# One routed-attention and SoLU kernel, its hand-written order rewritten from the first scores on

## The chip, the cores and the metric

The kernel runs on one core of one Trainium2 chip. The metric is device time in microseconds (us) of one execution; the runs of the kernel before gave 222.96, 223.10 and 223.19, median 223.1. A profiled execution gives the instruction times that are used below.

## What is computed

```python
q_n, k_n, c_n = (each row divided by its norm)             # q, k, v: 4 x 8 x 768 x 64, centroids: 8 x 16 x 64
q_assign = argmax(q_n . c_n);  k_assign = argmax(k_n . c_n)   # 16 clusters a head
scores = (q @ k^T) / 8, and -1e9 where q_assign != k_assign
attn = softmax(scores) @ v                                  # -> x: 3072 tokens x 512
h = x @ w_in                                                # 512 -> 1024
solu = h * softmax(h)
ln = (solu - mean) / sqrt(var + 1e-6) * g_ln
out = ln @ w_out                                            # 1024 -> 512, float32
```

## The kernel before

There are 16 pairs of heads, written b.p (batch 0 to 3, pair 0 to 3). The mask is put into the score matmul: the 64 rows of q and k of a head get 16 more rows, the one-hot cluster of each token, so that a score in the right cluster is raised by a constant and the others vanish in the exponential. The rows of q and k with their one-hot rows stand in the tiles qk0 to qk5.

The kernel is a list of small steps with names. Those that matter here:

- ld, lv: loads of q or k, and of v (DMA, issued from SyncE's queue). ld2.1.1 is k of pair 2.1.
- tp and xa (pairs of batch 0 only): TensorE turns a tile of q or k, and VectorE or ScalarE copies it out of PSUM (L409). xt (the other batches): VectorE turns it (L427).
- ca b.p.i.hh: cast of q (i = 0) or k (i = 1) of one head of the pair to bf16 into qk; L453 or L455 on GpSimd and VectorE, L451 on ScalarE.
- cl, tb, mx, oh, ot: the clusters of a pair. A matmul gives the 16 products of each token (cl, L465 or L470), VectorE turns them back (tb, L479), takes the maximum (mx, L492), compares (oh, L504, for pairs 0.1 to 0.3 L498) and turns the result (ot, L514 or L511). For a pair of batch 0 these four follow each other on VectorE and each takes the result of the one before.
- pl b.p.i.part: four copies of that result into the one-hot rows of qk (L534, for pairs 0.1 to 0.3 L526). bl: a memset beside it (L543). cv: a cast of v (L552).
- S, E, V, N: scores of a bank of up to 512 columns (TensorE, L621), their exponential (ScalarE, L627), the product with v (TensorE, L644), the division by the sum (VectorE, L656 and L669). A unit of three banks is named by one number: S8.0, S8.1 and S8.2 are unit 8, the first of pair 0.3; unit 4 is the first of pair 0.1, unit 6 of pair 0.2. Three PSUM banks hold scores, so each S waits for the E three banks before; the first S of a pair also waits for its ca and pl.
- h, hm, ex, u, tu, y, bn, ag, at, al, sc, ou: the second half of the network for a tile of 128 tokens: x @ w_in (L730), maximum, exponential, product, turn by DMA, product with w_out (L794), variance, the scale on GpSimd (at, al), scaling of the result (sc, on ScalarE L809 or VectorE L811), store.
- su, sk, me, ce: w_out is centred once, early; su is one us of matmuls (L593).

The order on each engine is a table of words: a word is a kind of step and how many of that kind come next, and a word with = names one step out of its turn. AWAY names the steps that go to another engine than their kind's default. Each engine works through its list strictly in order, so that a step that waits holds everything behind it on its engine. `run` walks the five lists, and every step issues its instructions when its turn comes; semaphores between engines follow from the tiles.

```python
ORDER["SP"], ORDER["POOL"], ORDER["PE"], ORDER["DVE"], ORDER["ACT"]   # the five lists
first, eng = eng, self.AWAY.get(name, eng)                             # the engine of a step
```

Of the kernel before, what the change touches and what calls it, by code (L numbers as in the profile page):

```python
# [22 lines left out]
class Weave:  # L23
# [11 lines left out]
    ORDER["POOL"] = """
        po z ca2 pl2 cv bl zo =pl0.0.1.0.0 pl bl ca2 cv z ca2 cv =pl0.1.1.1 z pl ca =pl0.1.0.1 pl ca
        gs =ca0.3.0.1 =pl0.2.0.0 pl =ca0.3.1.0 pl ca pl cv pl z cv wi sg =wi2 wi2 =pl1.0.0.0
        =pl1.0.1.1 =ca1.0.0.1 ca2 =pl1.0.0.1 pl =ca1.1.1.1 bl =ca1.1.0.1 cv =ca1.1.1.0 pl2 at z cv
        al =cv1.1.1 =pl1.1.0.1 ca cv pl ca at al at =ca1.2.1.0 =pl1.2.1.1 =cv1.3.0 =pl1.2.0.0
        =ca1.2.1.1 pl2 al cv bl ca2 cv =ca1.3.1.0 at =ca2.0.0.0 =ca1.3.1.1 al ca =pl1.3.0.0  # L40
        =pl1.3.1.1 pl at pl ca2 pl =pl2.0.0.0 =pl2.0.0.1 pl al cv at ca cv =pl2.1.0.0 =ca2.2.0.0 al
        =ca2.1.1.1 =pl2.1.1.1 =ca2.2.1.1 =ca2.1.1.0 ca =ca2.3.1.1 at pl2 at al bl cv ca at
        =ca2.2.1.0 =pl2.2.1.1 pl =pl2.2.0.1 =cv2.2.0 cv pl bl ca =ca3.0.0.1 al2 at =pl2.3.1.1
        =ca3.0.1.1 ca =ca2.3.1.0 =pl2.3.0.0 =ca3.0.1.0 pl bl at ca =pl3.0.0.1 al cv =pl3.0.1.1 ca
        pl2 bl =ca3.1.1.0 cv ca cv =pl3.1.1.1 =ca3.2.0.1 al at al =ca3.3.0.0 =pl3.1.0.1 cv pl bl pl
        ca2 =pl3.2.0.1 ca =ca3.3.1.1 at al ca =cv3.3.0 =cv3.2.1 =cv3.3.1 at pl cv pl bl =pl3.3.0.1
        pl ca bl at al at al at3 al4 at3 al at al2 at al2
    """
    ORDER["PE"] = """
        wm tp fl3 cp fl2 tp2 cl tp fl10 cl fl8 S2 tp S cq tp S tp S tp S tp S2 tp S cl V S V2 S2 tp2  # L50
        S2 V3 tp S tp S tp S2 cl S2 V S V2 S gt S tp S3 V S V2 S cl S3 su S V S V2 S2 V S3 V2 S V2
        S3 V2 S2 V S V S cl S3 su S3 V3 S V S me S V S V S V2 S3 V2 S2 V2 S2 h S h S2 V S V h S V S
        V S h S2 h S V2 S V S V h S cl S V2 S h S V S2 V h S2 h S h S2 V3 S2 V3 S2 y3 S y S h S h S
        V3 S cl V S2 h2 S V2 S2 h S h S2 V2 S V S V S y V2 y S y2 h S h S2 V2 y S3 y2 S V S2 V3 S y
        S2 h S h cl S3 V4 S V y V S2 y h S y V S y h S3 V cl S V S V2 S2 V S h S h V S V3 S3 cl S2
        V2 y2 S y S V2 S2 y S V S h2 S h S V S h S V S V h y2 S3 V y V S h S h S y V h S3 V2 cl S h
        V h S cl S h S V2 S V2 S V S h S2 h V S h S y2 S2 V3 S y V S2 V S y h V S2 h S y S V2 S V S2
        h V y2 S2 V2 h S y S2 h2 V S2 V S cl V S V S V2 S h2 S cl S2 V S y V S V S y V y S2 V h y S
        h S2 cl S V S2 y4 V2 S2 V2 S y S2 V3 S V S y S2 y V S2 V2 S V S h S h S V S2 V h y S h S V S
        V S V S V h2 S y V S y S V S V S h S2 V h S V S V S y2 h S h S V S cl h S h S V2 S2 h S V2 h  # L60
        S y V y S2 h2 S2 V4 S h V h S y S V S y S2 h S h S V3 S h V S h y V S y S V S h S h S2 V S V
        y h S2 V2 y h V2 S3 h2 S2 V S V2 y2 S V S y h y h2 S h S2 V2 h V S V y S y S h y2 h2 S2 V y
        S y3 V h2 y h2 y3 V2 h2 y4 h2 ptx y4 h2 y3 h2 ptu y ptu y6 ptu y ptu y5
    """
    ORDER["DVE"] = """
        cn cb xa ca tb mx oh ot pl2 tb mx oh ot xa pl xa cf xa ca2 tb mx pl oh ot xa N xa cv tb mx
        oh gk ot xa pl N tb mx oh ot pl N cv pl cv N xt2 ca N tb mx oh sk ot N ce2 N ce4 N ce2 xt N
        hm xt N u tb mx oh N ot hm bn2 xt ag bl u N xt hm tb bn u bn N mx ag oh bn hm ot cv N sc u
        bn2 ag xt bn xt ag xt N hm tb mx oh xt N ot xt u bl bn xt tb N bn hm N mx tb oh ag ot u N xt
        mx oh bl ot bn hm N bn ag u xt2 bn hm xt tb u N tb mx cv oh bn ag hm N ot mx bn u oh bn ot N  # L70
        bn hm xt ag bn xt u ag N xt bn hm tb xt N mx tb oh ot u bn xt ag xt hm tb N mx cv mx u N oh
        bn oh N bn ot bn2 ag N ot xt hm ag sc N u bn2 ag xt hm N sc u ca tb bn hm mx oh u ot N hm bn
        ag bn u cv N bn hm N ag u bn hm N bn2 u N ag sc hm bn2 ag u bn N hm ag bn2 u bn ag N hm bn
        ag u bn2 hm sc N u ag bn2 hm tx ag sc u bn2 hm tu sc ag u2 bn2 ag sc2
    """
# [16 lines left out]
    AWAY.update(dict.fromkeys("""  # L92
        pl0.0.0.1.0 pl0.0.1.0.0 pl1.0.0.0 pl1.0.0.1 pl1.0.1.0 pl1.0.1.1 pl1.1.0.0 pl1.1.0.1
        pl1.1.1.0 pl1.1.1.1 pl1.2.0.0 pl1.2.0.1 pl1.2.1.0 pl1.2.1.1 pl1.3.0.0 pl1.3.0.1 pl1.3.1.0
        pl1.3.1.1 pl2.0.0.0 pl2.0.0.1 pl2.0.1.0 pl2.0.1.1 pl2.1.0.0 pl2.1.0.1 pl2.1.1.0 pl2.1.1.1
        pl2.2.0.0 pl2.2.0.1 pl2.2.1.0 pl2.2.1.1 pl2.3.0.0 pl2.3.1.0 pl2.3.1.1 pl3.0.0.0 pl3.0.0.1
        pl3.0.1.0 pl3.0.1.1 pl3.1.0.1 pl3.1.1.0 pl3.1.1.1 pl3.2.0.0 pl3.2.0.1 pl3.2.1.0 pl3.3.0.1
        pl3.3.1.0 pl3.3.1.1
    """.split(), "POOL"))
# [1180 lines left out]
```

## Time and profile before

| | |
|---|---|
| median of three runs | 223.1 us |
| the profiled execution's own time | 223.39 us |
| its span (first to last instruction) | 221.2 us |
| granted TensorE clock over the span | 0.997 |
| TensorE busy | 213.0 us, 96% |
| VectorE busy | 198.8 us, 90% |
| ScalarE busy | 194.0 us, 88% |
| GpSimd busy | 126.7 us, 57% |

In rows of the profile PE is TensorE's matmul, PEld its weight loads, DVE is VectorE, ACT ScalarE, POOL GpSimd, SP SyncE; L621 is line 621 of the kernel before. A row of the timeline has start, duration, engine, line, operation, what is written from what, how often, and in square brackets the idle time before it with what ended it. Three engines are nearly full, so the question in each stretch is which of them the others wait for. A matmul's end is modelled, so that a busy TensorE is not always TensorE at its peak.

### The profile page before, as it was taken

The numbers are of one execution on the slowest core, as the hardware profiler recorded it, in microseconds if no ns is written. First come the engines' busy times: TensorE is split into PE (matmuls) and PEld (weight loads), VectorE is DVE, ScalarE is ACT, GpSimd is POOL, SyncE is SP. The second block draws the span as 40 slices with busy tenths as digits, with TensorE's granted clock in tenths as the row PEclk, the third lists the DMA queues.
The fourth block names the chain that finished last, engine by engine and source line by source line (L and its number), as shares of the span: only waits on it lengthen the run. The fifth ranks groups of instructions, "written<-read, shape, count | busy, mean of one in ns | idle before, by whom it ended". The sixth has DMA issues, their size and how long they took to land.

```text
span 221.2 us, 6638 instructions
## 1 busy us (share of the span) xinstructions
PE 213.0 (96%) x2421; PEld 142.3 (64%) x2454; DVE 198.8 (90%) x354; ACT 194.0 (88%) x379; POOL 126.7 (57%) x245
## 2 busy tenths in 40 slices
...
GB/s 158 327 281 239 208 358 257 149 131 170 140 214 174 193 148 133 193 192 155 209 206 133 177 127 211 220 166 179 269 114 61 48 122 190 117 100 158 176 71 142
DMA packets 125679, 38.80 MB, mean 175 GB/s; under 512 B 115016, under 2 KB 121168, under 8 KB 125648
## 3 DMA queue, kind: packets, MB, share of 16 engines
...
q10 hardware_dynamic: 1744, 0.52, 1.0%
q8 instruction: 19, 0.31, 0.6%
...
## 4 chain that ended last, share of the span: by engine, by line
PE 79%; SPq 4%; DVE 4%; DMA 4%; POOL 2%; ACT 2%; issue 2%; POOLq 0%; DVEq 0%; ACTq 0%
PE sps L621 25%; PE hreg L730 17%; PE yps L794 16%; PE ops L644 14%; PE csc L470 4%; SPq L421 3%; DMA raw<-in_k_dram 2%; ACT e L627 2%; DMA raw<-in_q_dram 2%; PE hreg L402 1%; SPq L418 1%; POOL qk L526 1%; POOL qk L453 1%; PE hreg L794 1%; DVE cst L479 1%
## 5 line engine op out<-in xcount | busy, mean ns | idle before, releaser
L627 ACT ACTIVATE e<-sps 128x512 bf16<-128x512 f32 (+1 forms) x294 | 150.9, 601 | 6.5 <-PE sps L621 4.9
L621 PE MATMUL sps<-qk 80*128 80x256 bf16 (+5 forms) x636 | 99.0, 262 | 1.1 <-POOL qk L526 0.4
L621 PEld LDWEIGHTS <-qk 80*128 80x128 bf16 (+1 forms) x636 | 50.7, 97 | 34.3 <-issue 9.2
L644 PEld LDWEIGHTS <-e 128*128 128x128 bf16 x1152 | 51.6, 97 | 11.7 <-issue 1.9
L644 PE MATMUL ops<-v,e 128*128 128x65 bf16 x1152 | 56.9, 193 | 0.4 <-DVE x L669 0.4
L730 PE MATMUL hreg<-w_in_sb,xT 128*128 128x512 bf16 x176 | 51.2, 378 | 0.9
L794 PE MATMUL yps<-w_out_c,uT 128*128 128x512 bf16 x167 | 46.5, 378 | 0.9
L742 ACT ACTIVATE e_sb<-hreg,nmax 128x1024 bf16<-128x1024 f32 x24 | 26.9, 1122 | 8.0 <-DVE nmax L736 7.9
L736 DVE TENSOR_REDUCE nmax<-hreg 128x1 f32<-128x1024 f32 x24 | 29.1, 1213 | 4.7 <-PE hreg L730 4.6
L760 DVE BATCH_NORM_STATS2 bs<-u 128x6 f32<-128x512 bf16 x48 | 31.5, 676 | 0.2
L534 POOL COPY qk<-oht 32x384 f32<-32x384 f32 (+1 forms) x48 | 23.9, 498 | 12.7 <-DVE oht L514 8.7
L749 DVE TENSOR_TENSOR u<-e_sb,hreg 128x1024 bf16<-128x1024 bf16 (+1 forms) x25 | 29.1, 1167 | 1.2 <-ACT e_sb L742 1.0
L453 POOL CAST qk<-xt 64x768 bf16<-64x768 f32 (+1 forms) x30 | 24.5, 818 | 5.7 <-DVE xt L409 3.4
L455 POOL TENSOR_SCALAR qk<-xt 64x768 bf16<-64x768 f32 x26 | 21.8, 838 | 8.0 <-DVE xt L427 6.3
L794 PEld LDWEIGHTS <-uT 128*128 128x128 bf16 x200 | 18.1, 97 | 11.1 <-issue 0.3
L776 POOL TENSOR_SCALAR esq<-es,mv 128x1 f32<-128x1 f32 x24 | 8.9, 370 | 27.4 <-DVE mv L764 23.8
L427 DVE STREAM_TRANSPOSE xt<-raw 128x768 f32<-128x768 f32 x24 | 22.8, 956 | 0.9 <-DMA raw<-in_k_dram 0.9
L730 PEld LDWEIGHTS <-xT 128*128 128x128 bf16 x192 | 17.0, 97 | 8.7 <-DVE u L749 1.0
L669 DVE TENSOR_TENSOR x<-ops,den 128x256 bf16<-128x256 f32 (+1 forms) x39 | 18.9, 486 | 1.3
L770 POOL TENSOR_SCALAR es<-esum 128x1 f32<-128x1 f32 x24 | 5.9, 247 | 24.0 <-ACT e_sb L742 23.3
L552 POOL CAST v<-vf 128x384 bf16<-128x384 f32 x25 | 12.8, 518 | 3.8 <-DMA vf<-in_v_dram 3.0
L779 POOL TENSOR_TENSOR alpha<-esq,halves 128x1 f32<-128x1 f32 x24 | 13.6, 568 | 2.0
...
## 6 DMA issues: line engine op xcount, KB each, us to landing
...
```

The source lines that it names most:

```text
L427: nc.vector.transpose(xt[:], raws[b, p, i][:].rearrange("p j c -> p (j c)"))
L453: VEC[e].tensor_copy(dst, src)
L534: ins = VEC[e].tensor_copy(dst.bitcast(F32), src.bitcast(F32).unsqueeze(1) .to_broadcast([NB, 2, n // 2]))
L621: nc.tensor.matmul(sps_[n, k][:, c0:c0 + w], side(b, h // 2, 1, h % 2, keys)[r], side(b, h // 2, 0, h % 2, slice(s0 * P, s0 * P + w))[r])
L627: nc.scalar.activation(es[n, k][:, :w], sps_[n, k][:, :w], Act.Exp, scale=exp_scale, bias=-exp_scale)
L644: nc.tensor.matmul(opss[g][:, s, :VW], es[n, k][:, c0:c0 + P], v1[slot(b, h // 2)][:, h % 2, kt, :VW], start=(kt == 0), stop=(kt == n_t - 1))
L730: uses(nc.tensor.matmul(hreg[:, at(f, f2)[1], :], xTs[f][:, dc, :], w_in_sb[:, dc, f2 * FF2:(f2 + 1) * FF2], start=(dc == 0), stop=(dc == ...
L736: uses(nc.vector.tensor_reduce(ff[f, "nmax"][:], pair_of(f), axis=AXY, op=Alu.max, negate=True), *both(f))
L742: uses(nc.scalar.activation(ff[f, "e"][:], pair_of(f), Act.Exp, bias=ff[f, "nmax"][:], accum_out=ff[f, "esum"][:]), *both(f))
L749: uses(nc.vector.tensor_tensor(ff[f, "u"][:, at_], ff[f, "e"][:, at_], pair_of(f)[:, at_], op=Alu.mult), *banks)
L760: nc.vector.bn_stats(ff[f, "bs"][:, f2, :], ff[f, "u"][:, f2, :])
L794: ins = nc.tensor.matmul(dst, ff[f, "uT"][:, at(f, f2)[0] * (n_fc // 2) + c, :], w_out_c[:, fc, cols], start=(fc == chunks[0]), stop=(fc = ...
```

## The change

The five lists and AWAY are new; steps, buffers, tile sizes and the rules of waiting are the same. All five lists begin as before: TensorE's up to S0.1, VectorE's up to tb0.0.1 (at 9.45 us in the profile), ScalarE's up to E0.2, GpSimd's first six steps, SyncE's first 16. They also end as before: TensorE's from S90.0, VectorE's from N32, ScalarE's from E74.0 on. What moves between engines can be read in AWAY, from which the lines that differ are these (a step that is not named has its default engine: GpSimd for ca of whole tiles, cv, bl and the pl of pairs 0.1 to 0.3; VectorE for xa outside pair 0.0; ScalarE for sc).

```diff
     ORDER["POOL"] = """
-        po z ca2 pl2 cv bl zo =pl0.0.1.0.0 pl bl ca2 cv z ca2 cv =pl0.1.1.1 z pl ca =pl0.1.0.1 pl ca
+        po z ca2 pl2 =z4 bl zo sg cv pl bl ca =ca0.1.1.1 ca =z3 ca pl cv ca z pl =ca0.3.0.1 gs cv
...
     AWAY.update(dict.fromkeys("""
-        ca0.0.0.0.0 ca0.0.0.1.1 ca0.3.1.1 ca3.3.1.0 sc23.0 tu22.1 tu23.1 xa0.0.1.0 xa0.1.0.1
-        xa0.2.0.0 xa0.2.0.1 xa0.2.1.0 xa0.2.1.1 xa0.3.1.0
+        ca0.0.0.0.0 ca0.0.0.1.1 ca1.3.0.1 ca2.1.0.1 ca2.2.1.1 ca3.3.1.0 sc23.0 tu22.1 tu23.1
+        xa0.0.1.0 xa0.1.0.1 xa0.2.0.0 xa0.2.0.1 xa0.2.1.0 xa0.2.1.1 xa0.3.0.0
     """.split(), "ACT"))
     AWAY.update(dict.fromkeys("""
-        bl1.1 bl1.3 bl2.0 ca0.0.1.0.0 ca0.1.0.0 ca0.1.1.0 ca1.0.1.0 ca3.1.0.1 cv0.1.1 cv0.2.1
-        cv0.3.0 cv1.2.1 cv2.2.1 cv2.3.0 cv3.2.0 pl0.0.0.0.1 pl0.0.1.0.1 pl0.2.1.0 pl0.3.0.0
-        pl0.3.0.1 sc1 sc10 sc11 sc13 sc17 sc19 sc20 sc22 sc23.1 tu22.0
+        bl1.0 bl3.0 ca0.0.1.0.0 ca0.1.0.0 ca0.2.0.1 ca0.2.1.0 ca1.1.1.1 ca3.1.0.1 cv0.0.0 cv0.2.0
+        cv0.2.1 cv0.3.0 cv1.2.0 cv1.3.1 cv2.3.0 cv3.0.1 pl0.0.0.0.1 pl0.0.1.0.1 pl0.1.0.0 pl0.1.0.1
+        pl0.2.1.0 pl0.3.0.0 sc1 sc10 sc11 sc13 sc17 sc19 sc20 sc22 sc23.1 sc5 tu22.0
     """.split(), "DVE"))
```

Numbers behind a name in the rows below are buffer numbers; a line number of the kernel after is one less than that of the kernel before.

VectorE, pairs 0.1 and 0.2, before: from oh0.1 (the compare) and ot0.1 (the turn) to ot0.2.

```order
L498 TENSOR_TENSOR w_out_c_113<-cst_386,mx_406 128x12x2x16
L511 STREAM_TRANSPOSE w_out_c_113<-w_out_c_113 128x768
L409 COPY xt_469<-hreg_111 128x384
L656 RECIPROCAL den_480<-ops_378 128x6
L669 TENSOR_TENSOR x_479<-ops_378,den_480 128x2x3x64
L409 COPY xt_469<-hreg_111 128x384
L552 CAST v1_1_106<-vf_232 128x6x64
L479 STREAM_TRANSPOSE cst_513<-csc_496 128x384
L492 TENSOR_REDUCE mx_530<-cst_513 128x24
L498 TENSOR_TENSOR w_out_c_113<-cst_513,mx_530 128x12x2x16
L581 COPY g_ln2_115<-gps_549 128x8
L511 STREAM_TRANSPOSE w_out_c_113<-w_out_c_113 128x768
```

VectorE, the same stretch after: oh0.1 is the line behind mx_409, and its oh0.2 follows behind these rows.

```order
L491 TENSOR_REDUCE mx_409<-cst_392 128x24
L497 TENSOR_TENSOR w_out_c_113<-cst_392,mx_409 128x12x2x16
L452 CAST qk2_101<-xt_380 64x6x128
L510 STREAM_TRANSPOSE w_out_c_113<-w_out_c_113 128x768
L655 RECIPROCAL den_473<-ops_385 128x6
L668 TENSOR_TENSOR x_472<-ops_385,den_473 128x2x3x64
L408 COPY xt_485<-hreg_111 128x384
L525 COPY qk1_100<-w_out_c_113 16x2x3x64
L408 COPY xt_504<-hreg_111 128x384
L525 COPY qk1_100<-w_out_c_113 16x2x3x64
L478 STREAM_TRANSPOSE cst_527<-csc_495 128x384
L454 TENSOR_SCALAR qk2_101<-xt_435 64x6x128
```

Between the turn of pair 0.1 and the turn back of pair 0.2 the cast of v is gone, and two pl of pair 0.1 stand there; two casts of pair 0.2 stand inside the chain of four.

GpSimd, the same stretch before: from the first cast of pair 0.2 to the last pl of pair 0.2.

```order
L453 CAST qk2_101<-xt_375 64x6x128 x2
L552 CAST v1_1_106<-vf_232 128x6x64
L526 COPY qk1_100<-w_out_c_113 16x2x3x64
L1245 MEMSET v1_3_108 128x12x2
L526 COPY qk1_100<-w_out_c_113 16x2x3x64
L455 TENSOR_SCALAR qk2_101<-xt_433 64x6x128
L526 COPY qk1_100<-w_out_c_113 16x2x3x64 x2
L455 TENSOR_SCALAR qk2_101<-xt_433 64x6x128
L587 COPY w_out_c_113<-g_ln2_115 128x256
L453 CAST qk3_102<-xt_469 64x6x128
L526 COPY qk2_101<-w_out_c_113 16x2x3x64 x2
```

GpSimd, after: the same stretch and the rows up to the first pl of pair 0.3.

```order
L452 CAST qk3_102<-xt_485 64x6x128
L586 COPY w_out_c_113<-g_ln2_115 128x256
L551 CAST v1_1_106<-vf_232 128x6x64
L454 TENSOR_SCALAR qk3_102<-xt_504 64x6x128
L525 COPY qk2_101<-w_out_c_113 16x2x3x64
L452 CAST qk3_102<-xt_485 64x6x128
L525 COPY qk2_101<-w_out_c_113 16x2x3x64 x2
L454 TENSOR_SCALAR qk3_102<-xt_504 64x6x128
L525 COPY qk3_102<-w_out_c_113 16x2x3x64
```

GpSimd has given up two casts of pair 0.2 and two pl of pair 0.1, and has got the cast ca0.3.1.1, which ScalarE did before; it stands ahead of the first pl of pair 0.3.

VectorE in batch 1, before: from u4 over the turn of k of pair 2.1 (xt_2038) to N16 (den_2092 and the row behind it).

```order
L749 TENSOR_TENSOR u_1995<-e_sb_1944,hreg_111 128x1024
L543 MEMSET qk1_100 16x384
L760 BN_STATS bs_2035<-u_1995 128x6
L427 STREAM_TRANSPOSE xt_2038<-raw_1860 128x768
L479 STREAM_TRANSPOSE cst_2064<-csc_2020 128x384
L656 RECIPROCAL den_2092<-ops_1980 128x6
L669 TENSOR_TENSOR x_1427<-ops_1980,den_2092 128x6x64
```

VectorE, after: the turn of k of pair 2.1 is xt_2056, N16 starts at den_2090.

```order
L748 TENSOR_TENSOR u_1979<-e_sb_1959,hreg_111 128x1024
L759 BN_STATS bs_1997<-u_1979 128x6
L426 STREAM_TRANSPOSE xt_2020<-raw_1821 128x768
L478 STREAM_TRANSPOSE cst_2032<-csc_2022 128x384
L759 BN_STATS bs_1997<-u_1979 128x6
L426 STREAM_TRANSPOSE xt_2056<-raw_1867 128x768
L655 RECIPROCAL den_2090<-ops_1999 128x6
L668 TENSOR_TENSOR x_1426<-ops_1999,den_2090 128x6x64
```

The memset has gone to GpSimd, and the turn of k of pair 2.1 stands one turn back and one BN_STATS later. On SyncE's queue one quarter of the load of k of pair 2.0 has moved ahead of tu3, so that the four quarters of ld2.1.1 stand one issue nearer behind tu3.

More of the change, by code (lines that the diff above doesn't have):

```diff
@@ L35 @@
     ORDER["POOL"] = """
-        po z ca2 pl2 cv bl zo =pl0.0.1.0.0 pl bl ca2 cv z ca2 cv =pl0.1.1.1 z pl ca =pl0.1.0.1 pl ca
[L37 to L46, printed above, removed]
@@ L47 @@
-        pl ca bl at al at al at3 al4 at3 al at al2 at al2
+        po z ca2 pl2 =z4 bl zo sg cv pl bl ca =ca0.1.1.1 ca =z3 ca pl cv ca z pl =ca0.3.0.1 gs cv
+        =ca0.3.1.0 =pl0.2.0.0 ca pl2 ca pl z =pl0.3.0.1 pl cv =wi1 wi3 =pl1.0.0.1 pl ca =ca1.1.0.0
+        =pl1.0.0.0 =ca1.0.1.1 pl =ca1.0.1.0 ca2 cv at ca cv =cv1.1.1 al ca =pl1.1.0.1 at =pl1.1.0.0
+        =pl1.1.1.1 pl at ca cv =ca1.2.1.1 bl ca al =pl1.2.1.1 pl cv pl2 al =ca1.3.1.1 =ca1.3.1.0 bl
+        ca cv at al at =pl1.3.1.1 pl =pl1.3.0.1 pl bl =ca2.0.1.1 =ca2.0.1.0 cv al ca at pl
@@ new lines @@
+        =pl2.0.0.1 =pl2.0.0.0 pl bl ca cv pl al =ca2.1.1.1 =ca2.2.1.0 pl ca =pl2.1.0.1 =ca2.2.0.1 pl
+        ca cv =ca2.3.0.1 =ca2.3.0.0 at ca bl =cv2.2.0 cv at =pl2.2.0.1 =pl2.2.0.0 al =pl2.3.1.1
+        =pl2.2.1.1 pl bl pl ca pl bl al =ca3.1.1.0 cv at ca =ca3.0.0.1 al ca =pl3.0.0.0 =pl3.0.0.1
+        =pl3.0.1.1 at al cv pl at =ca3.1.0.0 ca =pl3.1.1.1 cv at ca al =ca3.2.0.1 al =ca3.3.0.0 cv
+        =pl3.1.0.1 pl2 at al =ca3.2.1.1 ca2 bl =pl3.2.0.1 ca =ca3.3.1.1 =cv3.3.0 =cv3.2.1 =cv3.3.1
+        at pl cv pl bl =pl3.3.0.1 pl ca cv bl at al at al at2 al2 at al2 at3 al at al2 at al2
@@ L55 @@
[L55 to L63, printed above, removed]
+        wm tp fl3 cp fl2 tp2 cl tp fl10 cl fl8 S2 cq S tp2 S2 tp S tp S tp2 S2 cl S V3 S tp S tp S2
+        V3 S tp2 S tp S2 cl S2 V S V2 S gt S tp S3 V3 S2 cl S3 su S2 V2 S2 V2 S4 V3 S V S3 V2 S V S
```

61 lines of the change are left out of this document (34 added, 27 removed).

## The prediction

> **What bounds the kernel now.** I read the page's totals and its chain first, then the busy time of each engine by stretch, then the timelines of TensorE, VectorE and GpSimd where TensorE stands idle.
>
> ```profile
> span 221.2 us, 6638 instructions
> PE 213.0 (96%) x2421; PEld 142.3 (64%) x2454; DVE 198.8 (90%) x354; ACT 194.0 (88%) x379; POOL 126.7 (57%) x245
> PE 79%; SPq 4%; DVE 4%; DMA 4%; POOL 2%; ACT 2%; issue 2%; POOLq 0%; DVEq 0%; ACTq 0%
> ```
>
> TensorE is nearly full and carries most of the chain, and its work is not changed. So only TensorE's idle time can be won, about 8 us with start and end, and any step can make more of it. The view by stretch says where:
>
> ```profile
> core 0: us, PE busy (x) PEld busy (x) DVE busy (x) ACT busy (x) POOL busy (x), PEclk, DMA share, GB/s
> 9.40:19.40 10.00, 9.83 (x104) 6.83 (x104) 9.57 (x21) 9.23 (x24) 8.04 (x17) 1.00 0.89 255
> 19.40:30.00 10.60, 9.86 (x122) 5.90 (x115) 10.23 (x20) 9.99 (x21) 8.86 (x14) 1.00 0.96 281
> 30.00:58.00 28.00, 27.68 (x379) 19.60 (x380) 26.27 (x47) 27.49 (x56) 15.53 (x26) 1.00 0.82 191
> 58.00:88.00 30.00, 29.72 (x342) 19.71 (x345) 27.64 (x48) 28.87 (x57) 22.15 (x40) 1.00 1.06 172
> 91.00:160.00 69.00, 68.23 (x791) 46.20 (x802) 64.32 (x113) 66.60 (x129) 46.86 (x84) 1.00 0.98 187
> ```
>
> From 9.4 to 30 VectorE is full (9.57 of 10.00, 10.23 of 10.60) and TensorE loses 0.74 us in the second of these rows: here VectorE sets the pace. From 30 to 58 ScalarE is full (27.49 of 28.00). Its steps in that stretch are the same in both orders, so a first exponential of pair 0.3 that comes later by some amount ends the stretch later by the same amount. From 58 on TensorE is full (29.72 of 30.00, 68.23 of 69.00) and hands the delay on to the end, except where it now stands idle and can do so no more. The granted clock is 1.00 in every row and plays no part.
>
> The place where pair 0.3 starts is S8.0, and it waits for a pl:
>
> ```profile
> 28.72 0.38 PE L621 MATMUL sps<-qk 80*128 80x256 bf16 x2
> 29.54 0.61 PE L621 MATMUL sps<-qk 80*128 80x256 bf16 x4 [0.44 <-POOL qk L526]
> ```
>
> That pl (GpSimd, 28.80, below) starts 0.07 us after ot0.3 ends on VectorE. So the end of ot0.3 is the number to work out.
>
> **Term 1: VectorE from tb0.0.1 to ot0.3.** Rows of VectorE, with the cast ca0.1.0.0 at 13.21 and ca0.1.1.0 at 13.67, a pl at 15.96, oh at 16.24, 21.96 and 26.83, xa0.3.0.0 at 18.27, cv0.1.1 at 19.86, pl0.2.1.0 at 24.55, ot0.3 at 27.75 and cv0.3.0 at 30.88:
>
> ```profile
> 9.45 0.38 DVE L479 STREAM_TRANSPOSE cst<-csc 128x192 f32<-128x192 f32 x1
> 10.25 0.36 DVE L504 TENSOR_TENSOR oh<-cst,mx 128x192 bf16<-128x192 f32 x1
> ...
> 13.21 0.54 DVE L453 CAST qk<-xt 64x768 bf16<-64x768 f32 x1
> 13.67 1.19 DVE L455 TENSOR_SCALAR qk<-xt 64x768 bf16<-64x768 f32 x1
> 14.78 0.56 DVE L479 STREAM_TRANSPOSE cst<-csc 128x384 f32<-128x384 f32 x1
> ...
> 15.96 0.25 DVE L534 COPY qk<-oht 32x192 f32<-32x192 f32 x1
> 16.24 1.09 DVE L498 TENSOR_TENSOR w_out_c<-cst,mx 128x384 bf16<-128x384 f32 x1
> ...
> 18.27 0.52 DVE L409 COPY xt<-hreg 128x384 f32<-128x384 f32 x1
> ...
> 19.86 0.99 DVE L552 CAST v<-vf 128x384 bf16<-128x384 f32 x1
> ...
> 21.96 1.10 DVE L498 TENSOR_TENSOR w_out_c<-cst,mx 128x384 bf16<-128x384 f32 x1
> ...
> 24.55 0.35 DVE L526 COPY qk<-w_out_c 16x384 f32<-16x384 f32 x1
> ...
> 26.83 0.88 DVE L498 TENSOR_TENSOR w_out_c<-cst,mx 128x384 bf16<-128x384 f32 x1
> 27.75 0.98 DVE L511 STREAM_TRANSPOSE w_out_c<-w_out_c 128x768 bf16<-128x768 bf16 x1
> ...
> 30.88 0.36 DVE L552 CAST v<-vf 128x384 bf16<-128x384 f32 x1
> ```
>
> And GpSimd beside them:
>
> ```profile
> 10.33 0.25 POOL L543 MEMSET qk<- 16x192 f32 x1
> ...
> 13.38 1.06 POOL L455 TENSOR_SCALAR qk<-xt 64x768 bf16<-64x768 f32 x1 [0.23 <-DVE xt L409]
> ...
> 15.22 1.70 POOL L453 CAST qk<-xt 64x768 bf16<-64x768 f32 x2
> ...
> 19.81 0.83 POOL L455 TENSOR_SCALAR qk<-xt 64x768 bf16<-64x768 f32 x1
> ...
> 21.83 0.83 POOL L455 TENSOR_SCALAR qk<-xt 64x768 bf16<-64x768 f32 x1
> ...
> 26.80 0.50 POOL L526 COPY qk<-w_out_c 16x384 f32<-16x384 f32 x1
> ...
> 28.80 0.69 POOL L526 COPY qk<-w_out_c 16x384 f32<-16x384 f32 x1 [0.40 <-DVE w_out_c L511]
> ```
>
> The two lists together show the port. The cast at 13.21 takes 0.54 alone; the one at 13.67 takes 1.19 and ends at 14.86, 0.42 after GpSimd's cast ends at 14.44. The oh at 16.24 ends at 17.33, 0.41 after GpSimd's 16.92; the one at 21.96 ends 0.40 after 22.66; the one at 26.83 ends 0.41 after 27.30; the cv at 19.86 ends 0.21 after 20.64. So casts, copies and oh on VectorE wait until GpSimd's instruction is over; tb, mx, ot and xa do not. Of the three oh (1.09, 1.10, 0.88), about 0.45 each is work and 1.7 in all is waiting.
>
> From 9.45 to 28.73 (27.75 + 0.98) VectorE has no gap over 0.1 us: 19.28 us. Now, by start to start of neighbouring rows:
>
> - Leaves VectorE in this stretch: ca0.1.1.0 1.11 (13.67 to 14.78), cv0.1.1 0.91, xa0.3.0.0 0.44, waits included: 2.46.
> - Comes to it: cv0.0.0 0.36, pl0.0.1.0.0 0.28, ca0.2.0.1 and ca0.2.1.0 0.46 each (13.21 to 13.67), pl0.1.0.0 and pl0.1.0.1 0.38 each, xa0.3.1.0 about 0.50: 2.82 if none waits.
> - Net without any port wait of the new ones: +0.36.
>
> Then the waits, walked along the two new lists. ca0.1.0.0 now stands directly behind pl0.0.1.0.0, when GpSimd has just got xa0.1.1.1 for its cast: it waits like the cast at 13.67, +0.65. pl0.0.1.0.1 meets a cast too, +0.2. oh0.1 meets ca0.2.0.0 as oh0.1 does now, a little less, 0.5 for 0.67. ca0.2.0.1 meets nothing, since GpSimd's next step waits for ot0.1. ca0.2.1.0 meets GpSimd's ca0.3.0.1, +0.65. oh0.2 meets nothing (GpSimd waits there for the step ahead of it on VectorE), -0.6; oh0.3 comes at the end of a pl, -0.4; the rest +0.2. Sum of waits: 0.65 + 0.2 - 0.17 + 0.65 - 0.6 - 0.4 + 0.2 = +0.5. So ot0.3 ends at 28.73 + 0.36 + 0.5 = 29.6. GpSimd then is within ca0.3.1.1, which ScalarE did before, and its pl0.3.1.0 ends near 30.4: S8.0 comes 0.9 later than 29.54. S6.0 comes later too, since its last pl (pl0.2.1.0, now ending at 24.90) stands behind the same chain, at about 26.9, and su0 with 1 us of matmuls is behind it on TensorE. ScalarE loses ca0.3.1.1 here, which is worth nothing, because the exponentials wait for S6.0 and S8.0.
>
> Both ends: with no waits at all the chain is 19.28 + 0.36 - 1.7 = 1.3 us shorter, of which S8.0 can take only its idle 0.44; with the waits of the three oh as now and three casts that wait 0.65 each it is 0.36 + 1.95 = 2.3 longer. I take +0.9, the walk's value.
>
> The Trainium skill (SBUF — State Buffer, Who interferes with whom) says that the pair of ports is a lock held for a whole instruction, that issue order decides who blocks, and that a VectorE instruction with two SBUF inputs contends only with a GpSimd instruction that reads SBUF. The oh at 10.25, which took 0.36 beside the memset at 10.33, agrees with the last; a cast beside a memset no row here shows, and if by the page's rule for casts cv0.0.0 waited for that 0.25, the term would be +1.1 and not +0.9.
>
> **Term 2: the idle time at 90.** VectorE holds N16 back while it waits for a load, and TensorE's V40.0 waits for N16:
>
> ```profile
> 86.37 0.69 DVE L760 BATCH_NORM_STATS2 bs<-u 128x6 f32<-128x512 bf16 x1
> 87.92 0.98 DVE L427 STREAM_TRANSPOSE xt<-raw 128x768 f32<-128x768 f32 x1 [0.86 <-DMA raw<-in_k_dram]
> ...
> 90.09 0.35 PE L644 MATMUL ops<-v,e 128*128 128x65 bf16 x6 [0.40 <-DVE x L669]
> ```
>
> After, a turn back (0.56 at 14.78) and a BN_STATS (0.69) stand ahead of that xt, and its load is one issue nearer: the 0.86 is covered. The memset left VectorE, the BN_STATS came ahead of N16. N16 is about 0.6 earlier and TensorE's 0.40 goes: -0.4 (bounds 0 and -0.4).
>
> **Term 3: ScalarE in batches 1 and 2.** It gets ca1.3.0.1, ca2.1.0.1 and ca2.2.1.1 and gives sc5 to VectorE.
>
> ```profile
> 24.71 0.84 ACT L451 ACTIVATE qk<-xt 64x768 bf16<-64x768 f32 x1
> L809 ACT ACTIVATE y<-yps,alpha 128x512 f32<-128x512 f32 x15 | 10.5, 697 | 3.9 <-PE yps L794 2.1 <-issue 1.2 <-POOL alpha L779 0.6
> ```
>
> 3 x 0.84 - 0.70 = 1.8 us more, where ScalarE has 1.1 us free from 58 to 88 and 2.4 from 91 to 160, and TensorE is the bound. TensorE has h and y to run while a bank waits. Bounds 0 and +0.6; I take +0.1. The other moves (bl, cv and the order of h, y and loads) lie beside work in these stretches; cover gone, a bl costs 0.25 to 0.4.
>
> **Sum:** +0.9 - 0.4 + 0.1 = +0.6 on the profiled execution's 223.39 (span 221.2 and 2.2 around it). The median is 0.3 below that execution, so I set it on the median: 223.7. A difference within 0.2% (0.45 us) is what a measurement here cannot tell from none.
>
> **Rivals.** *Faster: the collisions fall on GpSimd.* Where VectorE's instruction starts first, GpSimd waits (its cast at 13.38 took 1.06 for the 0.83 of the one at 19.81, with the cast of 13.21 ahead of it). If the new lists meet in that order, the chain is up to 1.3 shorter, S8.0 loses its 0.44, term 2 its 0.4, and TensorE's other losses in 19.4 to 30 some of the remaining 0.3: -1.0, 222.1. It decides once the waits on VectorE fall below 1.7 - 0.36 = 1.3 us. For it: GpSimd now has long waits for ot0.1 and for the copy behind gt, in which VectorE collides with nothing. Against: ca0.1.0.0 and ca0.2.1.0 each meet a GpSimd cast that was free to start before. The lock's rule on the page named above leads to this one as easily as to my walk: only the order of the starts differs. Chance 0.31.
>
> *No change:* S8.0 is late by 0.4 to 0.5 only, and term 2 gives it back, or the order of 58 to 160 does: 223.1, within 0.45. Chance 0.24.
>
> *Slower by more:* the three casts on ScalarE hold exponentials that TensorE has no h or y to cover, 3 x 0.84 less 0.70, on top of term 1: 223.1 + 0.9 + 1.8 - 0.4 = 225.4 at most, 224.6 with half of it. Against it: ScalarE's free time above. Chance 0.07.
>
> **The numbers.** My forecast has 0.38, its own range 223.5 to 224.2. Slower 0.38 + 0.07 = 0.45, same 0.24, faster 0.31. The range for 8 in 10 must take in the faster rival and the lower half of the last: 222.0 to 224.6.
>
> **What the profile after would show.** Right: ot0.3 ends at 29.3 to 29.9 and the first scores behind GpSimd's wait start near 30.4; VectorE's casts of ca0.1.0.0 and ca0.2.1.0 take about 1.1 each, oh0.2 about 0.45; V40.0 has no idle time ahead of it; ScalarE is full from 31 to 59. Wrong: those casts take 0.5 and S8.0 starts at 29.1 or before. A new idle time of TensorE over 0.4 us between 60 and 160 would make the forecast too low.

## The result and the profile after

The kernel after takes 224.65 us (median of 11 runs, 223.78 to 226.02), beside 222.96 for the kernel before in the same series (222.53 to 223.83): ratio 1.0074, 95% interval 1.0052 to 1.0097, so about 1.7 us slower. A second series gave 1.0065 (1.0041 to 1.0089). The forecast was 223.7. The profiled execution took 224.81 with a span of 222.7.

The page of the kernel after, its totals and its chain by engine:

```profile
span 222.7 us, 6672 instructions
PE 214.6 (96%) x2454; PEld 142.4 (64%) x2454; DVE 198.5 (89%) x358; ACT 195.0 (88%) x380; POOL 122.6 (55%) x240
PE 86%; DMA 5%; DVE 4%; issue 2%; ACT 1%; SPq 0%; DVEq 0%; ACTq 0%
```

GpSimd does 4.1 us less (122.6 for 126.7), ScalarE 1.0 more, VectorE nearly the same; the chain still runs mostly through TensorE. The busy totals of TensorE (213.0 and 214.6) cannot be compared: the profile of before has 2421 matmul records for 2454 weight loads, that of after 2454 of both. Busy time by stretch, kernel after:

```profile
core 0: us, PE busy (x) PEld busy (x) DVE busy (x) ACT busy (x) POOL busy (x), PEclk, DMA share, GB/s
9.40:19.40 10.00, 9.84 (x108) 7.32 (x109) 9.47 (x20) 9.29 (x24) 6.20 (x14) 1.00 1.04 317
19.40:30.00 10.60, 9.33 (x118) 5.35 (x110) 10.26 (x21) 8.94 (x20) 8.86 (x15) 1.00 0.88 215
30.00:58.00 28.00, 27.42 (x373) 19.59 (x372) 24.61 (x50) 27.49 (x56) 16.07 (x26) 1.00 0.84 188
58.00:88.00 30.00, 29.99 (x347) 19.72 (x344) 28.58 (x47) 29.51 (x58) 19.24 (x37) 1.00 0.91 175
...
136.00:148.00 12.00, 11.48 (x124) 7.13 (x123) 10.08 (x20) 10.57 (x21) 7.21 (x15) 1.00 1.08 235
```

and the last of these stretches in the kernel before:

```profile
136.00:148.00 12.00, 11.89 (x150) 8.26 (x150) 11.44 (x24) 11.83 (x24) 7.92 (x14) 1.00 0.93 200
```

TensorE loses 0.53 more from 19.4 to 30 (9.33 for 9.86) and 0.41 more from 136 to 148, where VectorE (10.08 for 11.44) and ScalarE (10.57 for 11.83) stand idle longer as well: there all three wait for something else.

VectorE after, the casts, oh and the last ot that term 1 speaks of (start, duration):

```profile
9.77 0.51 DVE L551 CAST v<-vf 128x384 bf16<-128x384 f32 x1
...
14.34 1.07 DVE L452 CAST qk<-xt 64x768 bf16<-64x768 f32 x1
...
16.59 0.75 DVE L497 TENSOR_TENSOR w_out_c<-cst,mx 128x384 bf16<-128x384 f32 x1
...
21.97 1.12 DVE L454 TENSOR_SCALAR qk<-xt 64x768 bf16<-64x768 f32 x1
...
23.58 0.56 DVE L497 TENSOR_TENSOR w_out_c<-cst,mx 128x384 bf16<-128x384 f32 x1
...
27.77 0.56 DVE L497 TENSOR_TENSOR w_out_c<-cst,mx 128x384 bf16<-128x384 f32 x1
...
28.36 0.98 DVE L510 STREAM_TRANSPOSE w_out_c<-w_out_c 128x768 bf16<-128x768 bf16 x1
```

GpSimd beside them:

```profile
9.81 0.25 POOL L542 MEMSET qk<- 16x192 f32 x1
...
14.12 1.98 POOL L454 TENSOR_SCALAR qk<-xt 64x768 bf16<-64x768 f32 x2 [0.80 <-DVE xt L408]
...
21.85 0.82 POOL L452 CAST qk<-xt 64x768 bf16<-64x768 f32 x1
...
28.77 0.83 POOL L454 TENSOR_SCALAR qk<-xt 64x768 bf16<-64x768 f32 x1
29.66 0.51 POOL L525 COPY qk<-w_out_c 16x384 f32<-16x384 f32 x1
```

The casts ca0.1.0.0 (14.34) and ca0.2.1.0 (21.97) each run into a GpSimd cast and take 1.07 and 1.12; oh0.2 and oh0.3 take 0.56, for 1.10 and 0.88 before. The last ot ends at 29.34, 0.6 later than before, and GpSimd is then within ca0.3.1.1. What TensorE sees of it, and of the two later places (V40.0 at 90.80, V64.0 at 143.05):

```profile
26.59 0.39 PE L620 MATMUL sps<-qk 80*128 80x256 bf16 x2 [0.55 <-DVE qk L525]
...
30.23 0.66 PE L620 MATMUL sps<-qk 80*128 80x256 bf16 x4 [0.22 <-POOL qk L525]
...
90.80 0.35 PE L643 MATMUL ops<-v,e 128*128 128x65 bf16 x6
...
143.05 0.54 PE L643 MATMUL ops<-v,e 128*128 128x65 bf16 x12 [0.42 <-DVE v L551]
```

S6.0 is 0.80 later than before (25.79, the fifth of the six matmuls that one row shows from 25.34 on) and S8.0 0.69 (29.54). V40.0 waits for nothing. V64.0 waits 0.42 for a cast on VectorE, and that cast for the load of v of pair 2.3 (lv2.3). In the kernel after, SyncE's queue and VectorE:

```profile
137.68 1.21 SPq L546 DMA_DIRECT2D vf<-in_v_dram  x1
...
142.63 0.36 DVE L551 CAST v<-vf 128x384 bf16<-128x384 f32 x1 [1.11 <-DMA vf<-in_v_dram]
```

and in the kernel before:

```profile
136.17 0.92 SPq L547 DMA_DIRECT2D vf<-in_v_dram  x1
...
140.69 0.35 DVE L552 CAST v<-vf 128x384 bf16<-128x384 f32 x1
```

The issue is 1.5 us later, and VectorE stands still for 1.11 with its oh and N queued behind the cast. The prediction had no term for this.

### The profile page after: what moved, and what is told of

Same layout as the page of the kernel before. It is cut to its first block, busy times and chain, and to the rows that moved or that the text cites. A ratio compares the mean times of both kernels' runs of the same rounds, so it can differ in the third digit from the quotient of the medians.

```text
span 222.7 us, 6672 instructions
## 1 busy us (share of the span) xinstructions
PE 214.6 (96%) x2454; PEld 142.4 (64%) x2454; DVE 198.5 (89%) x358; ACT 195.0 (88%) x380; POOL 122.6 (55%) x240
## 4 chain that ended last, share of the span: by engine, by line
PE 86%; DMA 5%; DVE 4%; issue 2%; ACT 1%; SPq 0%; DVEq 0%; ACTq 0%
PE sps L620 26%; PE hreg L729 18%; PE yps L793 17%; PE ops L643 15%; PE csc L469 4%; DMA vf<-in_v_dram 2%; DMA raw<-in_k_dram 2%; ACT e L626 1%; PE hreg L401 1%; DMA raw<-in_q_dram 1%; DVE xt L408 1%; PE hreg L592 1%; PE csc L464 1%; PE hreg L793 1%; DVE qk L454 0%
## 5 line engine op out<-in xcount | busy, mean ns | idle before, releaser
L729 PE MATMUL hreg<-w_in_sb,xT 128*128 128x512 bf16 x192 | 53.9, 379 | 0.0
L793 PE MATMUL yps<-w_out_c,uT 128*128 128x512 bf16 x184 | 49.2, 379 | 0.1
L533 POOL COPY qk<-oht 32x384 f32<-32x384 f32 (+1 forms) x47 | 23.2, 497 | 11.8 <-DVE oht L513 7.8
L452 POOL CAST qk<-xt 64x768 bf16<-64x768 f32 (+1 forms) x27 | 22.0, 816 | 12.0 <-DVE den L655 7.2
L775 POOL TENSOR_SCALAR esq<-es,mv 128x1 f32<-128x1 f32 x24 | 8.3, 348 | 22.0 <-DVE mv L763 19.4
L551 POOL CAST v<-vf 128x384 bf16<-128x384 f32 x24 | 12.3, 521 | 7.0 <-DMA vf<-in_v_dram 6.4
```

What stands on the lines that cost most here:

```text
L533: ins = VEC[e].tensor_copy(dst.bitcast(F32), src.bitcast(F32).unsqueeze(1) .to_broadcast([NB, 2, n // 2]))
L729: uses(nc.tensor.matmul(hreg[:, at(f, f2)[1], :], xTs[f][:, dc, :], w_in_sb[:, dc, f2 * FF2:(f2 + 1) * FF2], start=(dc == 0), stop=(dc == ...
L793: ins = nc.tensor.matmul(dst, ff[f, "uT"][:, at(f, f2)[0] * (n_fc // 2) + c, :], w_out_c[:, fc, cols], start=(fc == chunks[0]), stop=(fc = ...
```

## The experiments

Four places are in question: the front, the idle time at 90, SyncE's queue from 105 to 140, and the engines' order behind the front. All ratios are to the kernel before, run beside them; 0.001 is 0.22 us.

**The front put back, and the front alone.** The lists of both kernels are cut behind N3 (VectorE), cv0.3.1 (GpSimd), E11.2 (ScalarE), V8.1 (TensorE) and SyncE's 26th step.

```diff
 front_back:   lists = kernel before up to the cut + kernel after behind it
 front_alone:  lists = kernel after up to the cut + kernel before behind it
```

> The stretch up to pair 0.3 (VectorE up to N3, GpSimd up to cv0.3.1, ScalarE up to E11.2, TensorE up to V8.1, SyncE's first 26 steps) in the order and on the engines of the kernel before; everything behind it as in the kernel after. Theory A: the new order of the front costs 0.7 us through S8.0, 0.5 comes back at 90, and 1.1 is lost between 137 and 148, where the load of v of pair 2.3 stands late in SyncE's queue; the three add up. Then this kernel takes 224.65 - 0.7 = 223.9 to 224.0, S8.0 starts near 29.5, and V64.0 still waits 0.4 for the cast of v behind that load. Theory B (the rival): what ends last in the late part is the transfers, which do not depend on when the front ends; then the 0.7 of the front is swallowed there and the kernel takes 224.5 to 224.7. Theory C: the front costs all 1.7 and the rest nothing: 223.0.

> The same stretch in the order of the kernel after, everything behind it as in the kernel before. Theory A: 222.96 + 0.7 = 223.7, S8.0 near 30.3, V40.0 waits 0.4 as in the kernel before, V64.0 does not wait. Theory B: part of it is swallowed later, 223.0 to 223.3. Theory C: 224.6.

front_back 1.0029 (1.0011 to 1.0046), front_alone 1.0032 (1.0014 to 1.0051). S8.0 in front_back:

```profile
29.75 0.61 PE L620 MATMUL sps<-qk 80*128 80x256 bf16 x4 [0.43 <-POOL qk L525]
```

and in front_alone:

```profile
30.30 0.66 PE L620 MATMUL sps<-qk 80*128 80x256 bf16 x4 [0.22 <-POOL qk L525]
```

By the ratios the front alone costs 0.7 us, as theory A had it, and the rest of the change 0.6; the spans, shown below, divide it otherwise. Against theory A, front_alone had no idle time ahead of V40.0, though its late lists are those of the kernel before. In front_back the cast of lv2.3 waited 0.49 for its load, and TensorE lost 0.22 from 136 to 148 (11.78 busy of 12.00), less than the 0.4 of theory A.

**The port in the front: one cast moved behind one maximum.**

```diff
 ORDER["DVE"]
-  =pl0.1.0.1 xa pl tb ca mx gk oh xa ot N
+  =pl0.1.0.1 xa pl tb mx ca gk oh xa ot N
```

> The kernel after with one step of VectorE moved: the cast ca0.2.1.0 (1.12 us at 21.97) stands behind mx0.2 instead of behind tb0.2, so that it starts when the cast of GpSimd that it meets (21.9 to 22.7) is nearly over. Port theory: the cast takes 0.5 to 0.7 instead of 1.12, the turn of pair 0.2 and S6.0 come 0.4 earlier, S8.0 0.3 to 0.4 earlier, and the kernel takes 224.2 to 224.4. Rival (the cast takes 1.1 for itself, or GpSimd's pl of pairs 0.2 and 0.3 set the end whatever VectorE does): S8.0 at 30.2 as before the edit and 224.6.

Ratio 1.0039 (1.0020 to 1.0059). VectorE, GpSimd and TensorE of this kernel:

```profile
22.54 0.54 DVE L454 TENSOR_SCALAR qk<-xt 64x768 bf16<-64x768 f32 x1
...
21.85 0.82 POOL L452 CAST qk<-xt 64x768 bf16<-64x768 f32 x1
...
29.72 1.15 PE L620 MATMUL sps<-qk 80*128 80x256 bf16 x6 [0.22 <-POOL qk L525]
```

The same cast on the same engine takes 0.54 for 1.12, and S8.0 comes 0.51 earlier. The cast ends where it ended before (23.08 for 23.09), but the maximum, which needs no port, is now done by then. The port theory holds, and one place in a list is worth 0.51 of the 0.69 that the front lost. The kernel came out 0.4 below what was expected (223.82); its profiled execution had no wait ahead of V64.0 either, which may be the rest.

**The late load of v.** First, lv2.3 and tu9 ahead of the two stores ou6 and ou7:

```diff
 ORDER["SP"]
-  ld8 ou2 tu lv tu ld
+  ld8 lv tu ou2 tu ld
```

> The kernel after with two steps moved on SyncE's queue: the load of v of pair 2.3 (lv2.3) and the turn tu9 stand ahead of the two stores ou6 and ou7 instead of behind them. Theory A: the load is issued near 135.1 instead of 137.7 and lands near 140, the cast cv2.3.0 on VectorE and V64.0 do not wait, and 0.5 to 1.1 us are won: 223.5 to 224.1. Theory B, as far as it goes here (the DMA engines are full and the load lands no earlier, or the stores come back as a wait): 224.4 to 224.7. Theory C: no change, 224.6.

> Both edits together. Theory A: the sum, 224.65 - 0.7 - 0.5 to 1.1 = 222.8 to 223.4, so level with the kernel before or a little faster, since the idle time of TensorE at 90 stays away (its 0.5 is kept). Theory B: 224.0 to 224.5. Theory C: 223.0.

Ratios 1.0239 (1.0216 to 1.0262) and 1.0200 (1.0176 to 1.0225): a miss of all theories. ScalarE of the first:

```profile
141.22 0.69 ACT L808 ACTIVATE y<-yps,alpha 128x512 f32<-128x512 f32 x1 [2.70 <-DMA out_dram<-y]
```

A scaling of the result waits 2.70 for a store to free its y, and the exponentials stand behind it. The stores are no filler: each is a buffer that ScalarE needs. The kernel says nothing on lv2.3. So the other way, the load made later in the kernel before:

```diff
 ORDER["SP"]  (kernel before)
-  ou2 tu lv tu ld2 lv
+  ou2 tu2 ld lv ld lv
```

> The kernel before with one step of SyncE's queue moved: the load of v of pair 2.3 stands behind tu10 and the first quarter of the load of q of pair 3.3 instead of ahead of them, so that it is issued near 138.2 instead of 136.2, later than in the kernel after (137.7). Theory A (a late lv2.3 alone makes the loss at 143): it lands near 142.3, the cast behind it and V64.0 wait, TensorE loses 0.6 to 1.1, and the kernel takes 223.7 to 224.2. Rival (TensorE has h and y to run there, and the loss of the kernel after had another cause): 223.1 to 223.3.

Ratio 1.0053 (1.0035 to 1.0072). Its queue, VectorE and TensorE:

```profile
138.18 0.53 SPq L547 DMA_DIRECT2D vf<-in_v_dram  x1
...
142.81 0.36 DVE L552 CAST v<-vf 128x384 bf16<-128x384 f32 x1 [2.51 <-DMA vf<-in_v_dram]
...
143.23 0.54 PE L644 MATMUL ops<-v,e 128*128 128x65 bf16 x12 [2.05 <-DVE v L552]
```

A late lv2.3 alone can make such a loss, 1.2 us by the ratio (2.05 of idle time in the profiled execution). TensorE's h and y do not cover it. Then two kernels with the queue of the kernel after mended:

```diff
 ORDER["SP"]  v22_early: the load of v of pair 2.2 ahead of tx10
-  tx lv tx ou tu2 lv ld9 ou pl ld7 tu ld8 ou2 tu lv tu ld
+  tx lv2 tx ou tu2 ld9 ou pl ld7 tu ld8 ou2 tu lv tu ld
 ORDER["SP"]  late_queue_back: as in the kernel before from step 100 on
-  tx lv tx ou tu2 lv ld9 ou pl ld7 tu ld8 ou2 tu lv tu ld
+  tx lv2 tx tu2 ou ld10 ou ld8 pl tu ld6 ou2 tu lv tu ld2
```

> The kernel after with one step of SyncE's queue moved: the load of v of pair 2.2 (lv2.2) stands ahead of tx10, as in the kernel before, instead of behind tu7. Theory A': the queue gets late there, since it stands idle for tu6 until 111.4 in both kernels and the load's 0.6 of issue and its 384 KB then come after that idle time instead of before it. Then all loads from pair 3.0 on are issued 0.6 to 1.0 earlier, lv2.3 lands near 141.8, and the kernel takes 224.0 to 224.3. Rival: the wait within the loads (three issues of 1.6 to 2.0 instead of 0.6 us) only moves, and the time stays at 224.5 to 224.7.

> The kernel after with SyncE's queue from the loads of pair 2.3 on (its step 100 and all behind) in the order of the kernel before; all other lists as after. Theory A: the loss between 137 and 148 comes from the order of this queue, which brings the loads of pair 3.2 and of v of pair 2.3 about 1.5 us later. Then lv2.3 lands near 141, V64.0 does not wait, the idle time ahead of cl3.2 is under 0.2, and the kernel takes 223.6 to 224.1. Rival B: the queue is late because the transfer engines are full and the front is late; its order is worth nothing and the time stays at 224.5 to 224.7.

Ratios 1.0050 (1.0025 to 1.0074) and 1.0061 (1.0038 to 1.0085). SyncE and VectorE of v22_early:

```profile
105.70 1.06 SPq L546 DMA_DIRECT2D vf<-in_v_dram  x2
...
136.48 0.74 SPq L546 DMA_DIRECT2D vf<-in_v_dram  x1
...
141.33 0.35 DVE L551 CAST v<-vf 128x384 bf16<-128x384 f32 x1
```

With the load of 384 KB ahead of the queue's wait for tu6 instead of behind it, lv2.3 is issued 1.2 us earlier, and neither kernel waits at V64.0 in its profiled execution. How the edit does it is not shown: the first load behind tu7 is issued no earlier (113.50 for 113.54), but the eight loads from there on take 5.06 us of the queue for 6.89. And casts_back, below, issues lv2.3 as early without this edit. By the ratios the gain is 0.3 to 0.5 us against the first series of the kernel after and 0.1 to 0.3 against the second, and the intervals overlap: what the queue's order costs in the median is not settled.

The kernel after once more, to see whether the wait is there each time:

> The kernel after itself once more, for a second profiled execution. Its first runs spread over 2.2 us (223.8 to 226.0), those of the kernel before over 1.3, and three kernels with nearly its late lists showed no idle time ahead of V64.0. Theory A1 (the late load is a matter of chance: lv2.3 lands with so little room that some executions wait for it): median 224.2 to 224.8, and the wait of V64.0 is there only if this execution takes over 224.4. Theory A2 (the order makes lv2.3 late each time): the wait of about 0.5 is there whatever the time.

Ratio 1.0065; the profiled execution took 224.24 and waited again:

```profile
142.48 0.54 PE L643 MATMUL ops<-v,e 128*128 128x65 bf16 x12 [0.26 <-DVE v L551]
```

Neither theory is right as written: it waits in a cheaper execution too, but by a changing amount (0.26 and 0.42), and casts_back, whose front and queue are those of the kernel after, does not wait at all. cast_behind_max and the two kernels with the queue mended do not wait either. The load lands with hardly any room.

**Both helpful edits on the kernel after.**

> The kernel after with both edits that helped: the cast ca0.2.1.0 behind mx0.2 on VectorE, and the load of v of pair 2.2 ahead of tx10 on SyncE's queue. If they add up: 0.5 for the port wait and 0.4 for the queue, S8.0 at 29.7, no idle time ahead of V64.0, ratio to the kernel before 1.001 to 1.003 (223.3 to 223.9). If the first did all (an earlier front gives the late load its room): the ratio of the first alone, 1.004.

Ratio 1.0024 (1.0008 to 1.0041): they add up within the intervals, and still do not reach the kernel before.

**What is left behind the front.** Front and queue as before, only the engines' order behind the front as after; the front back with v22_early's edit; and the three casts back on GpSimd:

```diff
 front_queue_back: front_back, and SyncE's list of the kernel before from step 100 on
 front_back_v22:   front_back, and v22_early's edit
 casts_back, AWAY of the kernel after for ScalarE; on GpSimd behind ca1.3.1.0, ca2.1.1.1 and ca2.2.0.1:
-  ca1.3.0.1 ca2.1.0.1 ca2.2.1.1
```

> The front and SyncE's queue from the loads of pair 2.3 on as in the kernel before; what is left of the change is the order of TensorE, VectorE, ScalarE and GpSimd behind the front, with the three casts on ScalarE. Theory A (the change loses in the front and through the queue alone): ratio to the kernel before 0.999 to 1.001 (223.0 to 223.3), no idle time ahead of cl3.2 or V64.0. Rival C (the order of the engines behind the front costs by itself): 1.003 as with the front alone put back, 223.7.

> The front as in the kernel before, and of the queue only the load of v of pair 2.2 ahead of tx10 again. Theory A': this one load is what makes the queue late, so the ratio is that of the kernel with the whole queue put back, 0.999 to 1.002 (223.0 to 223.6). Rival: 1.003, since the other moves of the queue or of the engines cost it.

> The kernel after with the three casts ca1.3.0.1, ca2.1.0.1 and ca2.2.1.1 on GpSimd again, behind other casts of the same pairs, instead of on ScalarE. Term 3 of the prediction (they cost 0.1, since ScalarE has free time and TensorE other work): 224.4 to 224.7, ratio 1.006 to 1.007. Rival (the exponentials behind them are what ends last): up to 3 x 0.84 less, 222.8 to 223.9; with half of it 224.0.

Ratios 1.0020 (1.0007 to 1.0032), 1.0022 (1.0006 to 1.0037) and 1.0086 (1.0062 to 1.0109). The first leaves 0.4 that front and queue do not account for, and front_back_v22 as much. The third says that it is not the casts on ScalarE: taking them back wins nothing. casts_back has the front and SyncE's list of the kernel after; its profiled execution, the fastest of its six, shows:

```profile
136.38 1.04 SPq L546 DMA_DIRECT2D vf<-in_v_dram  x1
...
140.97 0.36 DVE L551 CAST v<-vf 128x384 bf16<-128x384 f32 x1
```

So with the same queue list lv2.3 is issued at 137.68 (after), 137.36 (after_again) or 136.38, and the last is as early as v22_early has it. Busy time by stretch of front_queue_back:

```profile
58.00:88.00 30.00, 30.00 (x346) 19.71 (x343) 28.59 (x48) 29.52 (x58) 19.41 (x37) 1.00 1.05 179
91.00:136.00 45.00, 45.00 (x522) 29.18 (x519) 42.27 (x70) 43.81 (x84) 28.93 (x52) 1.00 0.93 179
136.00:148.00 12.00, 12.00 (x149) 8.28 (x148) 10.90 (x22) 11.51 (x23) 7.72 (x15) 1.00 0.91 189
```

TensorE counts as busy throughout, 12.00 of 12.00 from 136 to 148 too. So the 0.4 is no idle time that this view shows. Half of it does not lie between the first and the last instruction at all. Each execution has its time and its span; the medians, beside the kernel before run with them, are:

| kernel | ratio of the times | span, us more than before | time outside the span, us |
|---|---|---|---|
| before (four series) | 1 | 0 | 2.13 to 2.16 |
| after (second series) | 1.0065 | 1.45 | 2.17 |
| front_alone | 1.0032 | 0.95 | 1.93 |
| front_back | 1.0029 | 0.25 | 2.34 |
| late_queue_back | 1.0061 | 1.35 | 1.81 |
| v22_early | 1.0050 | 1.05 | 2.12 |
| front_queue_back | 1.0020 | 0.20 | 2.33 |
| casts_back | 1.0086 | 1.55 | 2.42 |

A span in this table is good to some 0.4 either way, that of front_queue_back to 0.2. So the order of the engines behind the front costs about 0.2 in the span, which can hardly be told from nothing; the other 0.2 is time outside of it, and no run here shows what makes that. Within the span the front is the larger part of the loss, and putting the whole late queue back wins 0.1, far within the noise.

**The idle time at 90 by itself**, in the kernel before:

```diff
 ORDER["DVE"]  (kernel before)
-  u bl bn xt tb N bn hm
+  u bl bn tb bn N xt hm
```

> The kernel before with only the idle time at 90 taken away: on VectorE the turn back of pair 2.0, the second BN_STATS and N16 stand ahead of the turn of k of pair 2.1 (xt2.1.1), which waits for its load. Theory A (this alone is what the kernel after gains): V40.0 has no idle time ahead of it and the kernel takes 0.4 less than the kernel before, 222.6 to 222.7. Rival: the turn of k of pair 2.1 now ends 1.3 later and holds its clusters or the loads of pair 3.1 behind it, and the time stays at 223.0.

Ratio 0.9998 (0.9978 to 1.0018): nothing. The reason stands in the trace of v_load_late, whose lists up to 136 are those of the kernel before, unchanged. VectorE and TensorE there:

```profile
87.07 0.96 DVE L427 STREAM_TRANSPOSE xt<-raw 128x768 f32<-128x768 f32 x1
...
89.63 0.34 PE L644 MATMUL ops<-v,e 128*128 128x65 bf16 x6
```

The turn that waited 0.86 for its load in the profile of before waits for nothing here, and V40.0 neither. Of the three profiles with these late lists (before, v_load_late, front_alone) only the first has that idle time: it belonged to one execution, not to the order. The interval of the ratio still allows a gain of up to 0.5.

**A version that beats both.** The edit above, and a second one in the front, in two forms:

```diff
 before_two_edits   ORDER["DVE"]
-  xa cv tb mx oh gk ot xa pl N
+  xa cv tb mx xa oh gk ot pl N
 before_two_edits   ORDER["PE"]
-  V2 S gt S tp S3
+  V2 S tp gt S4
 before_cast_behind ORDER["DVE"]
-  xa cv tb mx oh gk ot xa pl N
+  xa tb cv mx oh gk ot xa pl N
```

> A candidate that would beat both kernels: the kernel before with the idle time at 90 taken away as in the run before, and in the front the copy xa0.3.1.1 moved ahead of oh0.2 on VectorE, into the time in which oh0.2 waits for GpSimd's cast (with its turn tp0.3.1.1 ahead of gt on TensorE). Port theory: oh0.2 takes 0.5 instead of 1.1, VectorE's chain to the turn of pair 0.3 is 0.5 shorter, S8.0 loses its 0.44 of idle time and starts at 29.1, V40.0 does not wait: 222.2 to 222.5. Rival (GpSimd's waits take the place): S8.0 at 29.5 and 223.0.

> A candidate that would beat both kernels: the kernel before with N16 ahead of xt2.1.1 as in the runs before, and the cast cv0.1.1 on VectorE behind tb0.2 instead of ahead of it (0.99 us at 19.86, of which 0.45 is a wait for GpSimd's cast, and the turn back needs no port). Port theory: the cast takes 0.5, mx0.2 and oh0.2 come 0.4 earlier, oh0.2 then meets the end of a pl instead of a whole cast, and the copy xa0.3.1.1, the clusters of pair 0.3 and S5.1 come 0.5 to 0.9 earlier: S8.0 at 29.1, ratio 0.996 to 0.998 (222.3 to 222.8). Rival (as with the copy moved ahead of oh0.2: the collisions only move to the next copies): 0.999 to 1.000.

before_two_edits: 0.9992 (0.9978 to 1.0007). VectorE, GpSimd and TensorE:

```profile
22.47 0.76 DVE L498 TENSOR_TENSOR w_out_c<-cst,mx 128x384 bf16<-128x384 f32 x1
...
24.28 0.66 DVE L526 COPY qk<-w_out_c 16x384 f32<-16x384 f32 x1
...
24.79 1.08 POOL L526 COPY qk<-w_out_c 16x384 f32<-16x384 f32 x2
...
29.57 0.61 PE L621 MATMUL sps<-qk 80*128 80x256 bf16 x4 [0.90 <-POOL qk L526]
```

oh0.2 is down from 1.10 to 0.76, but the pl behind it, 0.35 before, now takes 0.66 beside GpSimd's work: 0.31 of the 0.34 is given back, and S8.0 stays at 29.57. The rival was right: the collision moved. before_cast_behind: 0.9977 (0.9963 to 0.9991), 222.58 us, faster than both kernels:

```profile
20.21 0.48 DVE L552 CAST v<-vf 128x384 bf16<-128x384 f32 x1
...
21.18 0.81 DVE L498 TENSOR_TENSOR w_out_c<-cst,mx 128x384 bf16<-128x384 f32 x1
...
21.67 1.02 POOL L455 TENSOR_SCALAR qk<-xt 64x768 bf16<-64x768 f32 x1
...
28.87 0.61 PE L621 MATMUL sps<-qk 80*128 80x256 bf16 x4 [0.84 <-POOL qk L526]
```

The cast takes 0.48 for 0.99, since the turn back ahead of it needs no port and GpSimd's cast is nearly over by then. Now oh0.2 starts before GpSimd's next cast, and GpSimd waits (1.02 for 0.83). S8.0 starts 0.67 earlier. The edit at 90 alone gave nothing that can be measured, so the gain is put down to this one swap, which was not run without it.

## Why the prediction was wrong

- **Term 1 was right in mechanism and a little large.** The last ot was put at 29.3 to 29.9 and ended at 29.34; the first scores behind GpSimd's wait at 30.4, measured 30.23; the two casts at about 1.1, measured 1.07 and 1.12; oh0.2 at 0.45, measured 0.56. The delay of S8.0 is 0.69, not 0.9, and front_alone prices it at 0.7 us by its ratio (0.3 to 1.1) and 0.95 by its span: ScalarE and TensorE hand it on in full, as far as that tells.
- **The page on the port.** The Trainium skill (SBUF — State Buffer, Who interferes with whom) would have a cast wait for a memset. The row at 9.77 agrees in kind: 0.51 beside the memset at 9.81, for 0.36 alone, ended 0.22 after it. In size it is 0.15 at most, not the 0.25 of the memset that the +1.1 was worked out from.
- **Term 2 failed.** The step "TensorE's 0.40 goes: -0.4" is true of the two profiles, and its sum was then "set on the median". The two other profiles with these late lists do not have that idle time (v_load_late, front_alone), and taking it away alone gave 0.9998. Against the median the term is near 0 (0.5 won to 0.4 lost by the interval), and with 0 the forecast would have been 224.1.
- **Term 3 was right**, as far as can be measured: put at 0.1, and casts_back wins nothing.
- **"The other moves lie beside work" failed**, and with it the price of nothing that they had. With the front put back, terms 2 and 3 leave -0.3; front_back measured 0.6 more than the kernel before (0.2 to 1.0), 0.25 of it in the span. One cause is seen: the load lv2.3 came 1.5 late, and V64.0 waited 0.42 for it, 0.26 the second time. The text named the sign itself, a new idle time over 0.4 between 60 and 160. How much of the median this is, and how much the other moves, stays open, since the wait changes from one execution to the next.
- **TensorE's idle time was read too high.** The prediction had TensorE at 29.72 of 30.00 from 58 to 88. v_load_late, whose lists are the same up to 136, shows 30.00 there and 45.00 of 45.00 from 91 to 136, where the profile of before has 44.51. The 33 matmul records that the profile of before lacks can make this difference; TensorE has next to no slack there.
- **Sum after the runs:** 0.7 for the front and 0.6 for all that lies behind it by the ratios, 0.95 and 0.25 by the spans; the change costs 1.5 to 1.7. The remaining 0.2 to 0.4 is within the noise, or belongs to both halves together.
- **Rivals.** "Faster" asked that the collisions fall on GpSimd; two of them fell on VectorE. "Slower by more" came nearest in time, but by luck: the cause it gave, the casts on ScalarE, is not there.
